# Places for the last z2 tiles, the rounding of the next tile's rows ahead of the norm, and the totals behind the third product, in one stage of an adaLN, S4 and gMLP kernel

## The chip, the cores and the metric

The kernel runs on one core of a Trainium2 chip. The time is the device time of one execution, in microseconds (us). Three runs of the kernel before took 1779.18, 1784.16 and 1779.81 us; their median is 1779.81 us. Smaller is better.

## The reference, cut to what matters

```python
h = _layernorm(x) * (1 + ca) + sa
x = x + ga * _A_ref(h, ...)              # S4: a long convolution along the 2048 rows
h = _layernorm(x) * (1 + cb) + sb
z = _gelu(einsum("bsd,df->bsf", h, w_in))        # 2048 x 576 by 576 x 4608
z1 = z[..., :Fh];  z2 = _layernorm(z[..., Fh:])  # Fh = 2304
g = einsum("ts,bsf->btf", w_sp, z2) + b_sp       # 2048 x 2048 by 2048 x 2304
x = x + gb * einsum("bsf,fd->bsd", z1 * g, w_out)
```

All arrays are float32. The kernel makes the large products of pairs of f16 numbers: a value is rounded to f16 ("hi"), and what is left over is rounded to f16 again ("lo"). The product by w_sp is made with fewer multiplications out of sums and differences of blocks, which is why half of z2's even tiles hold differences.

## The kernel before, in words

The program has three stages in a row: `ssm` (the S4 convolution and the first residual, about the first 440 us), `phase_a` (z2, up to about 683 us) and `phase_b` (z1, the product by w_sp, the product by w_out and the residual).

Phase A goes over the 2048 rows in 16 tiles b of 128 rows. The steps of one tile are small methods, and each puts its work on one engine:

- `turn(b)`: TensorE transposes the normalised rows n of tile b by five products into the PSUM tile `pt`, of which there is one.
- `turn_hi(b)`: ScalarE rounds `pt` to f16, into half of the tile `nt` (two instructions). `turn_lo(b)`: VectorE writes what is left over into the other half (two instructions), and GpSimd sends `nt` to DRAM for phase B (the transfer n_d). Three buffers `nt` take turns.
- `z2_mm(b, h)`, h = 0 to 4: the product of `nt` by 512 columns of w_in (256 for h = 4), 14 matmuls into a PSUM tile `pz`, of which there are six.
- `z2_gelu(b, h)`: ScalarE takes the gelu of `pz` into columns of the z2 tile, 128 x 2304 in float32. The z2 tile is taken from its pool at h = 0; before, three buffers take turns under the one name z2.
- `z2_stats(b, c)`: VectorE's statistics of 384 columns. `roots(b, x)`: VectorE's aggregation and a chain of 15 or so small instructions for the reciprocal root, for z2's tile b and for the rows of tile x. It ends with r and nm, the factor and the shift of the norm.
- `z2_diff(b)`, even tiles: VectorE subtracts one half of z2 from the other. `z2_norm(b)`: ScalarE applies the norm, in two instructions of 1152 columns on even tiles and one of 2304 on odd ones. `z2_store(b)`: two transfers from GpSimd's queue, z_d, send the tile to DRAM; when they have landed the place of the tile is free.
- `ln2_rows(b)`, `ln2_stats(b)`: VectorE's norm of the rows that a later tile will transpose.

Beside these the loop carries lists of side work for other weights, called by `do(b, k)`: loads, ScalarE's roundings, VectorE's sums and left-overs. The list PE holds products for totals, two matmuls of one column each into a `pz` tile, from which VectorE works out a scale (`sc`): `win_scale` at b = 1, 3, 5, 7, 9, `scales_sp` at 7 and `scales_out` at 14. Side loads `xz` bring blocks of w_sp, whose differences VectorE makes in place.

Each engine runs its instructions of phase A in the order in which the code issues them: `self.tied` wraps the engines so, and therefore all of them carry line 132, that of the wrapper. So an instruction that waits holds up all that stands behind it on its engine. For b above 2, the order in loop b before is, shortly: z2_mm(b, 0); gelu(b, 0); statistics of tile b-1's last columns; roots(b-1); diff; norm(b-1); ln2_rows(b+2); totals; z2_mm(b, 1); turn(b+1); gelu(b, 1); store(b-1); statistics; turn_hi(b+1); turn_lo(b+1); z2_mm(b, 2) and so on. For b = 3 this means that the first tile whose rounding stands behind a norm is tile 4; tiles 2 and 3 have it ahead.

After the loop come the statistics, roots, norm and store of tile 15, and phase A's buffers are handed back. Phase B begins with six units of z1 (`z1_unit`, matmuls L1415, gelu L1420). Then comes the first group of g_products (L1450 to L1452), whose operands `zset` are built from z2 as it lies in DRAM: loads `raw`, sums on VectorE (L1081 to L1083), hi on ScalarE (L1129), lo on VectorE (L1130). `g_unit` (L1465) adds its products up on VectorE, `out_products` (L1502 to L1505) is the product by w_out. Phase B's tiles lie where phase A's lay, and each waits for the last reader of what was there. In the built program the three z2 places lie at bytes 132544, 141760 and 150976 of a partition; The second and third tile z1 that phase B takes begin at bytes 134176 and 130080, 4096 bytes each, and so lie over the first place; its tiles gt and z1b begin at 138272 and 142368 and lie over the end of the first place and over the second. The first tile z1 lies elsewhere. Nothing of phase B lies at 150976. Before, tiles 12 and 15 are at the first place, 11 and 14 at the second, 13 at the third.

Of the kernel before, what the change touches and what calls it, by code (L numbers as in the profile page):

```python
# [9 lines left out]
F32 = mybir.dt.float32  # L10
# [12 lines left out]
FH = 2304  # L23
# [775 lines left out]
class Mlp:  # L799
# [419 lines left out]
    def z2_gelu(self, b, h):  # L1219
        n = min(512, FH - 512 * h)  # L1220
        if h == 0:
            self.zs[b] = self.zp.tile([128, FH], F32, name="z2")
            self.bz[b] = self.ap.tile([128, 6, 6], F32, name="bsz")
        self.nc.scalar.activation(self.zs[b][:, 512 * h:512 * h + n], self.pzs.pop((b, h))[:, :n], AF.Gelu_apprx_tanh,
                                  scale=self.wcol(5 + h, INV_IN))
# [24 lines left out]
    def phase_a(self):  # L1250
        self.prods, self.z1s, self.n2, self.bsp, self.gbs, self.wfs = {}, {}, {}, {}, {}, {}
        ap = self.ap = self.pool(self.c2, "ap", 2)
        cpa = ExitStack()
        self.pa = self.pool(cpa, "pa", 6, space=PSUM)
        self.ps1 = lambda: self.pa.tile([128, 512], F32, name="pz")
        self.zp = self.pool(self.c2, "zp", 3)
        self.wp = self.pool(self.ctx, "wp", 7, side="right")

        self.fp = self.pool(self.ctx, "fp", 1, side="right")
        self.wso = ap.tile([128, 4, 10, 128], F16, name="wso", bufs=1)  # L1260
        self.nc, plain = self.tied, self.nc
        self.nc.vector.memset(self.wso[64:, :, 9], 0.0)

        LD, PE, A0, A1, V0, V1 = range(6)
        sides = [[[] for _ in range(6)] for _ in range(17)]

        def side(b, k, fn, *a):
            sides[b][k].append((fn, a))

        def do(b, k):  # L1270
            for fn, a in sides[b][k]:
                fn(*a)

        for q in range(5):
            side(2 * q, LD, self.side_load, q)
            side(2 * q + 1, A0, self.side_sum, q)
            side(2 * q + 1, PE, self.win_scale, q)
            side(2 * q + 1, A1, self.side_hi, q)
            side(2 * q + 1, V1, self.side_last, q)
            side(2 * q + 1, V1, self.side_lo, q, 0)  # L1280
            side(2 * q + 2, V0, self.side_lo, q, 1)
        for h in range(2):
            side(1, LD, self.bsp_load, ap, h)
            side(2, A0, self.norm_bsp, h)
        for i in range(8):
            side(2 + i // 2, A1, self.wsp_load, 0, i, ap)
            side(3 + i // 2, A0, self.norm_sp, 0, i)
        for i in range(12):
            side(6 + i // 2, A1, self.out_load, ap, i)
            side(7 + i // 2, A0, self.norm_out, i)  # L1290
        for i in range(6):
            side(12 + i // 2, A1, self.wsp_load, 1, i, ap)
            side(13 + i // 2, A0, self.norm_sp, 1, i)
        side(13, V1, self.sums_out)
        side(14, PE, self.scales_out)
        side(6, V1, self.sums_sp, 0)
        side(7, PE, self.scales_sp, 0)
        side(11, PE, self.scales_gate, 0)
        for i in range(7):
            side(9 + i, V0, self.wsp_sums, i)  # L1300
            side(9 + i, A1, self.wsp_hi, 0, i)
            side(9 + i, V1, self.wsp_lo, 0, i)
            side(8 + i, V1, self.block_load, 0, i)
        side(10, LD, self.z1_rows, 0)
        side(11, LD, self.bias_load, 0)
        for f in (0, 9, 1):
            side(12, LD, self.z1_load, 0, f)

        self.turn(0)
        self.turn_hi(0)  # L1310
        self.x1_load(4)
        self.turn_lo(0)
        self.start_lo(3)
        do(0, LD)
        self.z2_mm(0, 0)
        self.start_sum(4)
        self.z2_gelu(0, 0)
        self.z2_mm(0, 1)
        self.win_scale(9)
        self.start_hi(4)  # L1320
        self.z2_gelu(0, 1)
        self.ln2_rows(1)
        self.z2_mm(0, 2)
        self.start_lo(4)
        self.z2_gelu(0, 2)
        self.z2_mm(0, 3)
        self.turn(1)
        self.turn_hi(1)
        self.z2_gelu(0, 3)
        self.turn_lo(1)  # L1330
        self.z2_mm(0, 4)
        self.ln2_stats(2)
        self.roots(x=2)
        self.ln2_rows(2)
        self.z2_stats(0, 0, 1, 2, 3)
        self.z2_gelu(0, 4)
        self.ln2_stats(3)
        self.z2_stats(0, 4)
        for b in range(1, 16):
            do(b, LD)  # L1340
            self.z2_mm(b, 0)
            do(b, A0)
            self.z2_gelu(b, 0)
            self.z2_stats(b - 1, 5)
            if b in (1, 2):
                do(b, PE)
                self.z2_mm(b, 1)
                self.turn(b + 1)
                self.z2_gelu(b, 1)
                self.turn_hi(b + 1)  # L1350
                self.turn_lo(b + 1)
            self.roots(b - 1, b + 2 if b + 2 < 16 else None)
            if b % 2:
                self.z2_diff(b - 1)
            self.z2_norm(b - 1)
            if b + 2 < 16:
                self.ln2_rows(b + 2)
            if b + 4 < 16:
                self.x1_load(b + 4)
            if b > 2:  # L1360
                if b > 3:
                    do(b, PE)
                self.z2_mm(b, 1)
                if b + 1 < 16:
                    self.turn(b + 1)
                self.z2_gelu(b, 1)
            self.z2_store(b - 1)
            do(b, V0)
            self.z2_stats(b, 0, 1)
            if 3 < b + 1 < 16:  # L1370
                self.turn_hi(b + 1)
                self.turn_lo(b + 1)
            self.z2_mm(b, 2)
            if b == 3:
                do(b, PE)
            self.z2_gelu(b, 2)
            do(b, A1)
            self.z2_mm(b, 3)
            self.z2_stats(b, 2, 3)
            self.z2_gelu(b, 3)  # L1380
            if b + 3 < 16:
                self.ln2_stats(b + 3)
            do(b, V1)
            self.z2_stats(b, 4)
            self.z2_mm(b, 4)
            self.z2_gelu(b, 4)
        cpa.close()
        self.z2_stats(15, 5)
        self.roots(15)
        self.z2_norm(15)  # L1390
        self.z2_store(15)
        self.nc = plain
        self.c2.close()
# [334 lines left out]
```

## Time and profile before

| | us |
|---|---|
| three runs | 1779.18, 1784.16, 1779.81 |
| profiled execution, its own time | 1783.02 |
| its span | 1781.2 |
| TensorE busy (matmuls) | 1693.0 |
| VectorE busy | 1119.1 |
| ScalarE busy | 785.2 |
| GpSimd busy | 223.9 |

The profile shows one execution. Its own time is 1.8 us over the span, for what lies before the first and behind the last instruction, and 3.2 us over the median of the runs. PE is TensorE, PEld its weight loads, DVE is VectorE, ACT ScalarE, POOL GpSimd and SP SyncE. PEclk is the share of its full clock that TensorE was granted. A timeline row gives start and length in us, engine, line, operation and tiles, and in brackets for how long the engine had stood idle and what ended that; a row of waits gives the sum in us, the number and the longest.

### The profile page before, as it was taken

The numbers are of one execution on the slowest core, as the hardware profiler recorded it, in microseconds if no ns is written. First come the engines' busy times: TensorE is split into PE (matmuls) and PEld (weight loads), VectorE is DVE, ScalarE is ACT, GpSimd is POOL, SyncE is SP. The second block draws the span as 40 slices with busy tenths as digits, with TensorE's granted clock in tenths as the row PEclk, the third lists the DMA queues.
The fourth block names the chain that finished last, engine by engine and source line by source line (L and its number), as shares of the span: only waits on it lengthen the run. The fifth ranks groups of instructions, "written<-read, shape, count | busy, mean of one in ns | idle before, by whom it ended". The sixth has DMA issues, their size and how long they took to land.

```text
span 1781.2 us, 33976 instructions
## 1 busy us (share of the span) xinstructions
PE 1693.0 (95%) x14202; PEld 1195.6 (67%) x14202; DVE 1119.1 (63%) x2182; ACT 785.2 (44%) x1023; POOL 223.9 (13%) x350
## 2 busy tenths in 40 slices
PE   5688999997999999999999999999999999999999
PEld 1344555565545555877787777887778787787787
DVE  7988999858899996988783544483222274222322
ACT  5669999854576665555351322241211132011110
POOL 1321222342122110000000000000000000000000
PEclk8788999998999999999999999999999999999999
DMA  8457545799598887876654666562655572555520
GB/s 277 140 206 236 144 129 162 188 250 303 165 289 285 268 237 227 288 277 241 222 204 154 246 238 222 204 254 101 217 203 188 176 271 70 182 173 175 201 84 28
DMA packets 145866, 361.57 MB, mean 203 GB/s; under 512 B 23296, under 2 KB 59008, under 8 KB 143792
## 3 DMA queue, kind: packets, MB, share of 16 engines
q1 hardware_dynamic: 103104, 167.30, 29.7%
q0 software_dynamic: 33120, 153.95, 25.8%
q10 hardware_dynamic: 9488, 38.16, 5.3%
q8 instruction: 111, 1.82, 0.4%
q14 instruction: 43, 0.35, 0.1%
HBM read 256.86 MB, written 93.05 MB: 196 GB/s over the span
## 4 chain that ended last, share of the span: by engine, by line
PE 59%; DVE 10%; issue 6%; DMA 4%; ACT 3%; SPq 0%; POOL 0%; ACTq 0%; DVEq 0%; POOLq 0%
PE ps L1452 10%; PE ps L1450 10%; PE ps L1451 10%; PE ps L1415 9%; PE pz L132 5%; PE ps L1505 3%; PE ps L1502 3%; PE ps L1504 3%; PE pk L132 2%; DVE zset L1130 2%; ACT z L132 1%; DVE gt L1465 1%; DMA gbs<-in_w_out 1%; DVE bsz L132 1%; DMA zset<-set_d 1%
## 5 line engine op out<-in xcount | busy, mean ns | idle before, releaser
L1450 PE MATMUL ps<-wsp,zset 128*128 128x256 f16 x2016 | 549.5, 273 | 6.3 <-DVE gt L1465 3.7
L1452 PE MATMUL ps<-wsp,zset 128*128 128x256 f16 x2016 | 549.5, 273 | 3.5 <-DVE zset L1130 3.4
L1451 PE MATMUL ps<-wsp,zset 128*128 128x256 f16 x2016 | 549.5, 273 | 0.0
L132 PE MATMUL pz<-wz,nt 128*128 128x512 f16 (+1 forms) x1120 | 224.7, 361 | 4.7 <-ACT nt L132 4.7
L1465 DVE SCALAR_TENSOR_TENSOR gt<-ps,sc,bsp 128x512 f32<-128x512 f32 x33 | 24.8, 750 | 316.4 <-PE ps L1452 316.4
L1415 PE MATMUL ps<-n2q,wf 128*128 128x512 f16 x1008 | 223.1, 379 | 0.0
L1450 PEld LDWEIGHTS <-zset 128*128 128x128 f16 x2016 | 197.5, 98 | 33.3 <-DVE gt L1465 4.3
L1452 PEld LDWEIGHTS <-zset 128*128 128x128 f16 x2016 | 197.3, 98 | 27.8 <-DVE zset L1130 4.9
L1451 PEld LDWEIGHTS <-zset 128*128 128x128 f16 x2016 | 197.3, 98 | 25.9
L132 PEld LDWEIGHTS <-nt 128*128 128x128 f16 x1120 | 110.1, 99 | 110.9 <-ACT nt L132 5.5
L1415 PEld LDWEIGHTS <-wf 128*128 128x128 f16 x1008 | 98.6, 98 | 111.7
L1427 POOL DMA_DIRECT2D zset<-set_d x96 | 50.8, 529 | 973.8 <-PE ps L1452 960.9
L1420 ACT ACTIVATE z<-ps,sc 128x512 f32<-128x512 f32 x56 | 37.9, 681 | 284.6 <-PE ps L1415 274.9
L1504 PE MATMUL ps<-wout,z 128*128 128x288 f16 x448 | 127.6, 286 | 0.0
L1505 PE MATMUL ps<-wout,z 128*128 128x288 f16 x448 | 127.6, 286 | 0.0
L1502 PE MATMUL ps<-wout,z 128*128 128x288 f16 x448 | 126.0, 286 | 0.9 <-ACT ot L1512 0.9
L1465 DVE SCALAR_TENSOR_TENSOR gt<-ps,sc,gt 128x512 f32<-128x512 f32 (+1 forms) x165 | 112.1, 696 | 5.4
L1130 DVE TENSOR_TENSOR zset<-raw,zset 128x1024 f16<-128x1024 f32 x48 | 58.7, 1224 | 84.3 <-ACT zset L1129 84.3
L1129 ACT ACTIVATE zset<-raw 128x1024 f16<-128x1024 f32 x48 | 50.3, 1050 | 95.8 <-PE ps L1452 55.5
L1520 DVE TENSOR_TENSOR ot<-ot,ps 128x288 f32<-128x288 f32 x31 | 14.0, 453 | 78.3 <-ACT ot L1512 78.3
L369 PE MATMUL ps<-ln_x,r1t 128*128 128x288 f32 x128 | 42.6, 491 | 19.2 <-ACT kab L437 8.0
L1512 ACT ACTIVATE ot<-ps 128x288 f32<-128x288 f32 x32 | 12.8, 408 | 106.2 <-PE ps L1502 88.1
(356 smaller groups left out, 2864.0 us busy)
## 6 DMA issues: line engine op xcount, KB each, us to landing
zset<-set_d POOLq DMA_DIRECT2D x96, 896.0 KB, 4.9
set_d<-zset ACTq DMA_DIRECT2D x36, 896.0 KB, 5.9
raw<-z_d SPq DMA_DIRECT2D x48, 512.0 KB, 4.7
wf<-win_d SPq DMA_DIRECT2D x72, 320.0 KB, 3.5
raw<-in_w_spT SPq DMA_DIRECT2D x43, 512.0 KB, 6.1
z_d<-z POOLq DMA_DIRECT2D x32, 576.0 KB, 7.9
u_d<-st1o POOLq DMA_DIRECT2D x16, 576.0 KB, 4.4
u<-u_d SPq DMA_DIRECT2D x36, 256.0 KB, 4.6
```

Source lines behind the costliest of these rows:

```text
L132: return self.tc.keep_in_program_order(f(*a, **k))
L1129: nc.scalar.activation(o[:, k, 0], t, AF.Copy)
L1130: nc.vector.tensor_tensor(o[:, k, 1], t, o[:, k, 0], op=ALU.subtract)
L1415: nc.tensor.matmul(pm.rearrange("p (t c) -> p t c", t=4), w[:, kw], self.n2[q][:, :, kn], start=i == 0, stop=i == len(Z1) - 1)
L1427: self.nc.gpsimd.dma_start(o, self.set_d[n // 4, n % 4])
L1450: T.matmul(pm, z[:, a, 0, c], w[:, b, 0], start=i + half == 0, stop=False, skip_group_check=True)
L1451: T.matmul(pm, z[:, a, 0, c], w[:, b, 1], start=False, stop=False, skip_group_check=True)
L1452: T.matmul(pm, z[:, a, 1, c], w[:, b, 0], start=False, stop=i == 7, skip_group_check=True)
L1465: V.scalar_tensor_tensor(dst, pm, inv, to, op0=ALU.mult, op1=ALU.add)
L1502: T.matmul(pl, p[:, 1, ts], w[:, 0, hs], start=st, stop=sp)
L1504: T.matmul(pa, p[:, 0, ts], w[:, 0, hs], start=st, stop=False)
L1505: T.matmul(pa, p[:, 0, ts], w[:, 1, hs], start=False, stop=sp)
```

## The change

The change does three things in phase A, and adds or drops no instruction.

First, the z2 tiles get names of their own, z20, z21 and z22, each with one buffer, and so a set place: tile b takes place b mod 3 up to tile 13, tile 14 takes place 0 and tile 15 place 2. In the built program the three places are the same three stretches of memory. After the change tiles 12 and 14 are at 132544, 13 at 141760, 11 and 15 at 150976. So tile 14 now follows tile 12 at its place (before: tile 11), and tile 15 follows tile 11 (before: tile 12).

Second, in the loop, the second product, the transposes of the next tile, the second gelu and `turn_hi(b+1)` stand ahead of the roots and the norm in all tiles (before: for b = 1 and 2 alone). `turn_lo(b+1)` stands behind roots and diff and ahead of norm and ln2_rows for b above 1 (before, for b above 2: behind two statistics of tile b).

Third, the totals of the PE list stand behind the third product for all b above 1 (before: ahead of the second product for b above 3).

```diff
@@ z2_gelu
-            self.zs[b] = self.zp.tile([128, FH], F32, name="z2")
+            self.zs[b] = self.zp.tile([128, FH], F32, name="z2%d" % (b % 3 if b < 14 else 2 * b - 28))
@@ phase_a
-        self.zp = self.pool(self.c2, "zp", 3)
+        self.zp = self.pool(self.c2, "zp", 1)
@@ phase_a, the loop over b
             self.z2_gelu(b, 0)
             self.z2_stats(b - 1, 5)
-            if b in (1, 2):
+            if b == 1:
                 do(b, PE)
-                self.z2_mm(b, 1)
+            self.z2_mm(b, 1)
+            if b + 1 < 16:
                 self.turn(b + 1)
-                self.z2_gelu(b, 1)
+            self.z2_gelu(b, 1)
+            if b + 1 < 16:
                 self.turn_hi(b + 1)
+            if b == 1:
                 self.turn_lo(b + 1)
             self.roots(b - 1, b + 2 if b + 2 < 16 else None)
             if b % 2:
                 self.z2_diff(b - 1)
+            if 2 < b + 1 < 16:
+                self.turn_lo(b + 1)
             self.z2_norm(b - 1)
             if b + 2 < 16:
                 self.ln2_rows(b + 2)
             if b + 4 < 16:
                 self.x1_load(b + 4)
-            if b > 2:
-                if b > 3:
-                    do(b, PE)
-                self.z2_mm(b, 1)
-                if b + 1 < 16:
-                    self.turn(b + 1)
-                self.z2_gelu(b, 1)
             self.z2_store(b - 1)
             do(b, V0)
             self.z2_stats(b, 0, 1)
-            if 3 < b + 1 < 16:
-                self.turn_hi(b + 1)
-                self.turn_lo(b + 1)
             self.z2_mm(b, 2)
-            if b == 3:
+            if b > 1:
                 do(b, PE)
             self.z2_gelu(b, 2)
```

The difference of the two programs on ScalarE, in loop b = 3 (z_5052 is the z2 of tile 2, z_5199 that of tile 3, and nt<-pt is the rounding of tile 4's rows; nm and r belong to tile 2's norm):

```order
-L132 ACTIVATE z_5199<-pz,sc 128x512
-L132 ACTIVATE z_5052<-z_5052,nm_5221,r_5220 128x1152
-L132 ACTIVATE z_5052<-z_5052,r_5220 128x1152
-L132 ACTIVATE z_5199<-pz,sc 128x512
-L132 ACTIVATE nt<-pt 128x512
-L132 ACTIVATE nt<-pt 128x128
+L132 ACTIVATE z_5199<-pz,sc 128x512 x2
+L132 ACTIVATE nt<-pt 128x512
+L132 ACTIVATE nt<-pt 128x128
+L132 ACTIVATE z_5052<-z_5052,nm_5246,r_5245 128x1152
+L132 ACTIVATE z_5052<-z_5052,r_5245 128x1152
 L132 ACTIVATE z_5199<-pz,sc 128x512
```

The second gelu of tile 3 and the rounding of tile 4 have moved from behind the two instructions of tile 2's norm to ahead of them; every later tile shows the same move.

VectorE before, in loop b = 14, from the end of tile 13's roots on (nm belongs to tile 13, z_6949 is the z2 of tile 14, nt<-pt is turn_lo of tile 15, sc<-pz begins what is worked out from the total of `scales_out`, and xz is a block of w_sp):

```order
L132 SCALAR_TENSOR_TENSOR nm_6972<-mvx,r_6971 128x1
L132 COPY sc<-pz 128x1
L132 TENSOR_SCALAR p2e<-sc 128x1
L132 TENSOR_SCALAR p2e<-p2e 128x1
L132 TENSOR_SCALAR sc<-p2e 128x1
L132 TENSOR_SCALAR sc<-sc 128x1
L132 TENSOR_TENSOR xz<-xz 128x256 x3
L1024 TENSOR_TENSOR sc<-sc 128x1
L132 TENSOR_TENSOR xz<-xz 128x256
L132 BN_STATS bsz<-z_6949 128x6 x2
L132 TENSOR_TENSOR nt<-pt,nt 128x512
L132 TENSOR_TENSOR nt<-pt,nt 64x128
```

and VectorE after, at the same place in the program (nm_6997 is tile 13's):

```order
L132 SCALAR_TENSOR_TENSOR nm_6997<-mvx,r_6996 128x1
L132 TENSOR_TENSOR nt<-pt,nt 128x512
L132 TENSOR_TENSOR nt<-pt,nt 64x128
L132 TENSOR_TENSOR xz<-xz 128x256 x4
L132 BN_STATS bsz<-z_6949 128x6 x2
L132 COPY sc<-pz 128x1
L132 TENSOR_SCALAR p2e<-sc 128x1
L132 TENSOR_SCALAR p2e<-p2e 128x1
L132 TENSOR_SCALAR sc<-p2e 128x1
L132 TENSOR_SCALAR sc<-sc 128x1
```

turn_lo of tile 15 has moved up to right behind the roots, past the block's differences and the two statistics, and the scale from the totals has moved down behind them.

On TensorE only the totals move, by two products, in the loops b = 5, 7, 9 and 14. On GpSimd's queue the transfer n_d of each tile from 4 on now stands ahead of the two z_d of the tile two before it. SyncE's order and the whole of phase B are as they were.

## The prediction

> **What bounds the kernel now.** I read the page first: how much of the span each engine works.
>
> ```profile
> span 1781.2 us, 33976 instructions
> PE 1693.0 (95%) x14202; PEld 1195.6 (67%) x14202; DVE 1119.1 (63%) x2182; ACT 785.2 (44%) x1023; POOL 223.9 (13%) x350
> ```
>
> TensorE (PE) works 95% of the span, so a reordering can win only what TensorE loses by waiting or by a low clock. The change touches phase A alone, from about 440 to 683 us, and through its end the start of phase B. So next the windows of TensorE, cut where it stood idle.
>
> ```profile
> core 0: us, PE busy (x), PEclk, DMA share, GB/s
> 440.00:497.40 57.40, 57.33 (x306) 1.00 0.59 191
> 497.40:501.10 3.70, 0.04 (x2) 0.87 0.71 201
> 501.10:510.10 9.00, 9.00 (x29) 0.67 0.96 316
> 693.20:696.80 3.60, 0.39 (x2) 1.00 0.00 0
> 696.80:800.00 103.20, 99.34 (x848) 1.00 0.79 280
> ```
>
> There is a hole in phase A, at 497.4, with a low granted clock in the 9 us behind it, and one at 693.2, where phase B's first set product waits. The timeline of TensorE names what ended the waits.
>
> ```profile
> 446.26 6.20 PE L132 MATMUL pz<-wz,nt 128*128 128x512 f16 x28
> 501.08 9.11 PE L132 MATMUL pz<-wz,nt 128*128 128x512 f16 x28 [3.66 <-ACT nt L132]
> 646.96 3.19 PE L132 MATMUL pz<-wz,nt 128*128 128x512 f16 x14 [0.32 <-ACT nt L132]
> 674.88 18.29 PE L1415 MATMUL ps<-n2q,wf 128*128 128x512 f16 x84
> 695.40 0.28 PE L1450 MATMUL ps<-wsp,zset 128*128 128x256 f16 x1 [2.23 <-ACT zset L1129]
> 696.80 0.28 PE L1452 MATMUL ps<-wsp,zset 128*128 128x256 f16 x1 [1.00 <-DVE zset L1130]
> ```
>
> The two phase A waits are for ScalarE's rounding of the next tile's rows (tiles 4 and 14); those in phase B are for the hi and then the lo half of the first set. ScalarE's timeline says why these came late.
>
> ```profile
> 497.48 1.35 ACT L132 ACTIVATE z<-z,nm,r 128x1152 f32<-128x1152 f32 x1 [2.47 <-DVE z L132]
> 500.45 0.75 ACT L132 ACTIVATE nt<-pt 128x512 f16<-128x512 f32 x2
> 682.26 2.31 ACT L132 ACTIVATE z<-z,nm,r 128x2304 f32<-128x2304 f32 x1 [5.44 <-DVE nm L132]
> 684.48 1.25 ACT L1420 ACTIVATE z<-ps,sc 128x512 f32<-128x512 f32 x2
> 692.99 0.69 ACT L1420 ACTIVATE z<-ps,sc 128x512 f32<-128x512 f32 x1 [7.26 <-DMA z_d<-z]
> 693.57 1.05 ACT L1129 ACTIVATE zset<-raw 128x1024 f16<-128x1024 f32 x1
> ```
>
> At 497.5 ScalarE stood idle for VectorE, did tile 2's norm, a gelu, and only then tile 4's rounding at 500.45. At the end it waits for VectorE's roots of tile 15, norms (682.26), does two gelus of z1, and waits 7.26 us for the store of tile 15, because the third gelu writes where tile 15 lies; the first set's rounding is queued behind it. So two engines set the seam: TensorE, which is done with z1 at 674.88 + 18.29 = 693.17, and the chain VectorE, norm(15), store, gelu, rounding, first lo at 696.7.
>
> VectorE itself is nearly never idle in phase A; this window has all engines, and the waits are all that VectorE has there.
>
> ```profile
> 466.00:682.00 216.00, 212.03 (x1111) 110.25 (x1110) 194.53 (x583) 144.07 (x211) 48.21 (x62) 0.98 0.81 255
> DVE bsz L132 <- ACT z L132: 4.0, 5, 1.3
> DVE xz L132 <- DMA xz<-in_w_spT: 1.8, 1, 1.8
> DVE nt L132 <- ACT nt L132: 1.4, 1, 1.4
> DVE wsp L132 <- ACT wsp L132: 0.7, 1, 0.7
> ```
>
> 194.53 us busy (third pair of numbers) and 4.0 + 1.8 + 1.4 + 0.7 = 7.9 us of named waits; the other 13.6 us go in steps between 583 instructions, which no reordering of these removes. So norm(15) can come earlier by a part of 7.9 us and no more.
>
> **The change part by part.** No instruction is added or removed, so every term is a wait.
>
> ```profile
> 481.26 1.02 DVE L132 TENSOR_TENSOR nt<-pt,nt 128x512 f16<-128x512 f32 x2 [1.40 <-ACT nt L132]
> 500.57 0.56 DVE L132 BATCH_NORM_STATS2 bsz<-z 128x6 f32<-128x384 f32 x1 [0.92 <-ACT z L132]
> 552.68 1.35 ACT L132 ACTIVATE z<-z,nm,r 128x1152 f32<-128x1152 f32 x1 [0.58 <-DVE z L132]
> ACT wso L132 <- DVE sc L132: 1.3, 1, 1.3
> ```
>
> *Rounding ahead of the norm, tile 4.* The second gelu and the rounding go into ScalarE's idle 2.47 us before 497.48: 0.69 for a gelu and 0.75 for the rounding are 1.44 us and fit there, so tile 4's hi is ready before TensorE wants it at 501.08 - 3.66 = 497.42. This removes 3.66 us idle and, as the hole goes, the slow stretch: 28 matmuls took 9.11 us there and 6.20 us at 446.26, so 2.91 us. By the Trainium skill, "TensorE: Matmul & The Clock Gate", section "What's actually happening", the array falls to half clock after about one idle window of some 3.4 us and is back after as much busy time; the trace agrees, with 3.66 us idle bringing 0.67 over the next 9 us and 2.23 us none of it. The lo half now stands behind roots and diff: VectorE's diff ended just before 497.48, and 1.0 us of lo follows; TensorE could wait for it between 0 and 1 us. I take 0, since hi products come first. With the 0.32 us at tile 14 TensorE's z1 units end 3.66 + 2.91 + 0.32 = 6.89 us earlier, at 686.28.
>
> *The same on VectorE.* turn_lo no longer comes behind statistics that wait for the late gelu. The first two rows above are the waits of that kind around tiles 3 and 4, and I let their 1.40 + 0.92 = 2.32 us go. ScalarE's spare time at a norm is under 1.44 us at one tile only, b = 7 (third row, 0.58 us), where VectorE may wait up to 0.86 us. At tile 15's rounding VectorE has the wait of 1.8 us for a block: turn_lo(15) waits in its place for about as long, and meanwhile the block comes. The bounds are 0 and all 7.9 us; I take 2.3, the two waits that the moved steps caused: norm(15) begins at 682.26 - 2.3 = 679.96.
>
> *The totals.* They go behind two more products on TensorE. A product takes 3.19 us, so the scale comes about 6.4 us later, and ScalarE's side rounding waits for it. Its users stand behind two gelus more, and VectorE's tiny chain behind statistics; I cost it at nothing; if that cover is gone, at the one wait of ScalarE for a scale that the trace shows in this stretch (fourth row), 1.3 us, in each of three loops (5, 7, 9).
>
> *GpSimd.* The transfer n_d now stands ahead of the two z_d. It waits for turn_lo, which is ahead of the norm, so nothing queues behind it that was ready; what it takes is hidden in the queue's long waits for the norm (the first three rows below).
>
> ```profile
> 646.32 2.01 POOL L132 DMA_DIRECT2D z_d<-z  x2 [11.51 <-ACT z L132]
> 673.52 2.00 POOL L132 DMA_DIRECT2D z_d<-z  x2 [10.51 <-ACT z L132]
> 685.02 2.02 POOL L132 DMA_DIRECT2D z_d<-z  x2 [9.49 <-ACT z L132]
> 686.04 6.84 DMA z_d<-z
> DMA to landing us min/median/max: 5.3/7.7/13.9
> ```
>
> *Set places.* The rows are the stores of tiles 12, 14 and 15, the second transfer of tile 15 from issue to landing, and the landings of all z_d from 472 to 690 us. z1's second tile now lies over tile 14's place. Its second transfer, issued a microsecond after the first, lands near 674.5 + 7.7 = 682.2, less the 2.3 us that VectorE gained: before the third gelu of z1, and that wait of 7.26 us goes. Then norm(15) at 679.96, the two gelus at 682.2, the third at 683.4, the rounding at 683.9 in place of 693.57: 9.7 us earlier. The first lo follows at the same distance, 3.23 us, at 687.1 in place of 696.80.
>
> *Sum.* TensorE is done with z1 at 686.28 and needs the first lo at 686.3 or so; it gets it at 687.1. TensorE gains 6.89 and its wait of 2.23 + 1.00 shrinks to about 0.8: in all 696.80 - 687.1 = 9.7 us. Behind that the order is the same, and the waits for lo halves from 700 to 900 us stay:
>
> ```profile
> PE ps L1452 <- DVE zset L1130: 2.4, 3, 1.3
> ```
>
> The profiled execution, 1783.02 us, becomes 1773.3; the median of the runs is 3.21 below the profiled one, so 1779.81 - 9.7 = **1770.1 us**. Bounds of this case: if VectorE gains nothing, 2.3 less (7.4 us, 1772.4); if it gains 3 or more, TensorE's 686.3 caps the start at 0.8 us more, and these 2.4 us might go too: 9.7 + 0.8 + 2.4 = 12.9 us, 1766.9.
>
> **The rivals.**
>
> *The place of tile 12 is not free in time.* gelu(14,0) writes over tile 12, whose second transfer, issued at about 647.3, landed 8.6 us later, the longest of these two:
>
> ```profile
> DMA to landing us min/median/max: 5.4/7.0/8.6
> 652.21 0.71 ACT L132 ACTIVATE z<-pz,sc 128x512 f32<-128x512 f32 x1
> ```
>
> The first row is of tile 12's transfers alone. gelu(14,0) ran at 652.21; it would now wait until 655.9. VectorE's wait for turn_lo(15) takes the place of the wait for the block, so my sum holds that much. With the longest landing of the stage, 13.9 us, it is 5.3 us more, VectorE and norm(15) come as much later, the rounding at 689.2, and the gain is 4.4 us: 1775.4. The Trainium skill, "Perfetto Trace Analysis", section "Identifying Performance Opportunities", says that gaps that repeat on the engine that should be full can mean too few buffers for the next tile; here that would be one gap, at tile 14, and no row of the kernel before shows ScalarE waiting for a z2 place. Chance 0.10.
>
> *The gain is given back or half made.* The first quarter of phase B is short of VectorE and of sets; set 3 needs tile 15's store, which moves by 2.3 us only, while TensorE wants it 9.7 us earlier. The read of z2 for a set takes 4.7 us:
>
> ```profile
> raw<-z_d SPq DMA_DIRECT2D x48, 512.0 KB, 4.7
> ```
>
> By my count the store lands at 685.02 - 2.3 + 1.0 + 6.84 = 690.6, set 3 is read by 695.3, its hi and first lo take the 3.23 us of set 0, 698.5, and the rest of it another microsecond. TensorE has three sets of 42 matmuls ahead of it, at 103.20 / 848 = 0.12 us each 15 us, so it wants set 3 at 702. If that fails, or if TensorE's hole at tile 4 stays, half is lost: 9.7 / 2 gives 1775.0; with the seam alone, 3.23 us, 1776.6. That is also the case in which the change doesn't do what it says. Chance 0.09.
>
> *Slower: VectorE waits for the rounding in every tile.* turn_lo now stands right behind roots (and diff), ahead of work that VectorE could do; if gelu and rounding come late there, because TensorE's second product or transposes or ScalarE's side work are late, VectorE loses up to 1.44 us a tile.
>
> ```profile
> ACT z L132 <- DVE nm L132: 31.7, 8, 5.4
> ACT z L132 <- DVE z L132: 29.7, 8, 8.7
> ```
>
> Against it: ScalarE waits 61.4 us in 16 norms, a mean of 3.8 us, so the room is there. With 12 tiles (b = 3 to 14) of 1.44 us and three loops of 1.3 us for the later totals it would cost 21.2 us of a VectorE that has no slack; less 2.3, norm(15) begins at 701.2, the rounding 3.94 us behind it as in my sum, at 705.1, 11.5 us later than before: 1791.3. It decides where the spare time at the norm is under 1.44 us in most tiles. Chance 0.07.
>
> **How the numbers follow.** My forecast has 0.74, the rivals 0.10, 0.09 and 0.07. The likeliest case's own range is 1766.9 to 1772.4; up to 1776.6 takes in the first two rivals and leaves out the slow one and what scatter there is. A measurement tells 0.3% from no change, 5.3 us here: faster means under 1774.5. So the two mild rivals are "same": 0.74 faster, 0.19 same, 0.07 slower.
>
> **What would show it.** Right: no wait of TensorE at tile 4 and clock 1.00 from 497 to 510; VectorE's waits in phase A near 5 us; the third z1 gelu with no wait for z_d; the first set product near 687 and the rest of phase B shifted whole. Wrong: a wait of ScalarE for z_d at tile 14 of more than 4 us, waits of VectorE for nt in many tiles, or new waits of TensorE for sets between 690 and 800 us.

## The result and the profile after

The changed kernel is slower, by about half a per cent: nine runs from 1784.16 to 1797.78 us with a median of 1791.86, against 1782.19 us for the kernel before in nine runs beside them; the ratio is 1.0051, 95% interval 1.0028 to 1.0074. The forecast was 1770.1 us and faster. Executions of one kernel scatter by 5 us and more to either side; and behind the S4 stage, which no edit touches, phase A began between 435.4 and 442.7 us in the twelve profiled executions. So below a stage is compared by distances inside an execution: from the transposes of tile 0 (line pt, the start of phase A on TensorE) to norm(15) on ScalarE, and to the first set product by a lo half on TensorE (the third set product, L1452 before and L1447 after).

The page of the changed kernel's profile, and behind it its windows of TensorE in phase A:

```profile
span 1787.0 us, 33982 instructions
PE 1696.9 (95%) x14202; PEld 1195.5 (67%) x14202; DVE 1117.7 (63%) x2182; ACT 785.2 (44%) x1023; POOL 223.8 (13%) x350
```

The windows, each with its length, TensorE's busy time and instructions, the granted clock, the share of the DMA engines and GB/s:

```profile
440.00:684.80 244.80, 232.39 (x1215) 0.99 0.80 235
504.90:516.70 11.80, 7.68 (x43) 1.00 0.91 300
516.70:524.60 7.90, 7.89 (x30) 0.78 0.61 164
```

Every engine works nearly as long as before; TensorE 3.9 us longer. From 440 us to z1's first matmul it takes 244.8 us in place of 234.9. The timeline of TensorE after shows the holes:

```profile
439.61 0.76 PE L132 MATMUL pt<-ident,n 128*128 128x128 f32 x5
493.71 10.75 PE L132 MATMUL pz<-wz,nt 128*128 128x512 f16 x56
516.71 7.89 PE L132 MATMUL pz<-wz,nt 128*128 128x512 f16 x28 [4.13 <-ACT nt L132]
563.85 9.41 PE L132 MATMUL pz<-wz,nt 128*128 128x256 f16 x42 [3.04 <-ACT z L132]
612.88 4.49 PE L132 MATMUL pz<-wz,nt 128*128 128x512 f16 x20 [1.32 <-DVE nt L132]
626.80 6.22 PE L132 MATMUL pz<-wz,nt 128*128 128x512 f16 x28 [1.32 <-ACT nt L132]
704.21 0.27 PE L1447 MATMUL ps<-wsp,zset 128*128 128x256 f16 x1
```

The hole at tile 4 is gone: TensorE runs on from 493.71. But there is one at tile 5, of 4.13 us and with a low clock behind it (0.78), and others follow. TensorE's step from one tile's transposes to the next is about 14.2 us for most tiles, but 20.1 and 20.2 us where the holes of 4.13 and 3.04 us lie, and 15.7 us twice later. The waits of VectorE and ScalarE over phase A and the seam tell why:

```profile
DVE nt L132 <- ACT nt L132: 18.6, 5, 8.0
ACT z L132 <- DVE nm L132: 18.0, 6, 5.4
ACT z L132 <- DVE z L132: 15.9, 3, 8.7
ACT wsst L132 <- DMA wsst<-in_w_spT: 15.2, 8, 4.7
ACT wsst L132 <- DMA wsst<-in_w_out: 15.1, 8, 3.8
ACT wso L132 <- DVE sc L132: 8.5, 4, 3.3
ACT wso L132 <- DMA wst<-in_w_in: 6.4, 1, 6.4
```

VectorE, which had no time to lose, now waits 18.6 us for ScalarE's roundings (1.4 before). ScalarE waits about half as long at its norms, and in place of that 30.3 us for the loads wsst, the blocks of weights whose squares it sums at the top of each loop (1.4 before), and 6.4 us for one more side load, wst (none before). One lap of what follows from that, as ScalarE's, SyncE's, VectorE's and again SyncE's timelines have it between tiles 4 and 5 (wsst is loaded from w_sp, x1t is the row buffer that ln2_rows frees, n<-x1t is ln2_rows):

```profile
498.78 0.34 SPq L132 DMA_DIRECT2D x1t<-x_d  x1
499.21 3.62 SPq L132 DMA_DIRECT2D wsst<-in_w_spT  x2
508.05 1.06 ACT L132 ACTIVATE wsst<-wsst 128x1024 f32<-128x1024 f32 x1 [2.96 <-DMA wsst<-in_w_spT]
513.87 1.06 ACT L132 ACTIVATE wsst<-wsst 128x1024 f32<-128x1024 f32 x1 [4.66 <-DMA wsst<-in_w_spT]
514.92 1.25 ACT L132 ACTIVATE z<-pz,sc 128x512 f32<-128x512 f32 x2
516.06 0.76 ACT L132 ACTIVATE nt<-pt 128x512 f16<-128x512 f32 x2
516.85 1.02 DVE L132 TENSOR_TENSOR nt<-pt,nt 128x512 f16<-128x512 f32 x2 [5.85 <-ACT nt L132]
517.90 0.82 DVE L132 SCALAR_TENSOR_TENSOR n<-x1t,mvx,mrow 128x576 f32<-128x576 f32 x1
518.75 0.34 SPq L132 DMA_DIRECT2D x1t<-x_d  x1
519.19 0.94 SPq L132 DMA_DIRECT2D wsst<-in_w_spT  x2
```

It is a ring. On SyncE the row load of tile b+4 stands ahead of the side loads, and it waits until ln2_rows(b+2) has read the buffer, so the side loads leave only then. Behind their squares on ScalarE stand both gelus and the rounding; turn_lo on VectorE waits for that; and behind turn_lo, since the change, stands the next ln2_rows, which frees the next row load. This lap took 518.75 - 498.78 = 20.0 us. The two laps behind it took 13.4 and 14.0 us (the next row loads leave at 532.17 and 546.20), the third 20.8 (566.95). TensorE's own step is 14.2 us, so even a quick lap leaves little room to make up for a slow one.

The ring does not say why this lap was slow. The loads did not leave late: before, the same pair left at 498.57, which is 60.0 us behind the first transposes, and after it left at 499.21, 59.6 us behind them. They landed late. The first row is SyncE's before; the two others are the landings of wsst that left between 496 and 515 us, four transfers before and two after:

```profile
498.57 0.90 SPq L132 DMA_DIRECT2D wsst<-in_w_spT  x2
DMA to landing us min/median/max: 5.1/5.7/6.8
DMA to landing us min/median/max: 8.8/10.4/12.0
```

The other slow lap began in the same way: its pair left at 546.65 and took 13.7 and 15.0 us to land (the pair of that loop before, 6.4 and 8.6), while the pairs in between took 5.6 to 7.5. So each of the two losses of some 6 us began with loads that landed slowly, and the new order of VectorE let them hold up the engine that has no time to lose. Why they landed slowly is not shown.

The seam went as forecast. ScalarE's timeline:

```profile
669.44 1.26 ACT L132 ACTIVATE z<-pz,sc 128x512 f32<-128x512 f32 x2 [3.33 <-DMA z_d<-z]
695.56 2.31 ACT L132 ACTIVATE z<-z,nm,r 128x2304 f32<-128x2304 f32 x1 [5.44 <-DVE nm L132]
697.77 1.82 ACT L1415 ACTIVATE z<-ps,sc 128x512 f32<-128x512 f32 x3
```

The third gelu of z1 follows the first two with no wait for a store, and TensorE runs into the first set product without one. But norm(15) stands 695.56 - 439.61 = 255.95 us behind the first transposes, before 682.26 - 438.61 = 243.65: 12.3 us later. The first lo product is 704.21 - 439.61 = 264.6 us behind them, before 696.80 - 438.61 = 258.2: the 12.3 us, less the 5.9 that the seam saved, are 6.4.

### The profile page after: what moved, and what is told of

Read it like the earlier page. It is cut to its first block, busy times and chain, and to the rows that moved or that the text cites. A ratio compares the mean times of both kernels' runs of the same rounds, so it can differ in the third digit from the quotient of the medians.

```text
span 1787.0 us, 33982 instructions
## 1 busy us (share of the span) xinstructions
PE 1696.9 (95%) x14202; PEld 1195.5 (67%) x14202; DVE 1117.7 (63%) x2182; ACT 785.2 (44%) x1023; POOL 223.8 (13%) x350
## 4 chain that ended last, share of the span: by engine, by line
PE 48%; DVE 5%; issue 5%; DMA 4%; ACT 1%; SPq 0%; ACTq 0%; DVEq 0%; POOLq 0%
PE ps L1445 9%; PE ps L1446 9%; PE ps L1410 9%; PE ps L1447 9%; PE ps L1500 3%; PE ps L1497 3%; PE ps L1499 3%; DVE zset L1130 2%; DVE gt L1460 1%; DMA zset<-set_d 1%; PE pz L132 1%; DMA raw<-z_d 1%; DMA gbs<-in_w_out 1%; ACT zset L1129 1%; DMA raw<-in_w_out 1%
## 5 line engine op out<-in xcount | busy, mean ns | idle before, releaser
L1447 PE MATMUL ps<-wsp,zset 128*128 128x256 f16 x2016 | 549.5, 273 | 3.0 <-DVE zset L1130 3.0
L132 PE MATMUL pz<-wz,nt 128*128 128x512 f16 (+1 forms) x1120 | 225.9, 361 | 11.9 <-ACT nt L132 7.0
L1447 PEld LDWEIGHTS <-zset 128*128 128x128 f16 x2016 | 197.2, 98 | 26.9 <-DVE zset L1130 4.1
L369 PE MATMUL ps<-ln_x,r1t 128*128 128x288 f32 x128 | 41.5, 480 | 20.1 <-issue 12.8
## 6 DMA issues: line engine op xcount, KB each, us to landing
u<-u_d SPq DMA_DIRECT2D x36, 256.0 KB, 4.6
```

The source lines that it names most:

```text
L132: return self.tc.keep_in_program_order(f(*a, **k))
L1447: T.matmul(pm, z[:, a, 1, c], w[:, b, 0], start=False, stop=i == 7, skip_group_check=True)
```

## The experiments

Theory RING is that turn_lo ahead of ln2_rows closes the ring above. Its rivals were that the later totals hold ScalarE up (TOTALS) and that n_d and z_d side by side crowd the DMA engines, so that loads land slowly (QUEUE). Each run was timed in five rounds against the kernel before.

| run | ratio to before, 95% interval | norm(15), us behind first transposes | first lo product, us behind them | VectorE waits for nt | ScalarE waits for wsst |
|---|---|---|---|---|---|
| before | | 243.7 | 258.2 | 1.4 | 1.4 |
| changed | 1.0051 (1.0028 to 1.0074) | 256.0 | 264.6 | 18.6 | 30.3 |
| 1 turn_lo put back | 0.9960 (0.9946 to 0.9974) | 245.1 | 256.1 | 0 | 11.9 |
| 2 totals put back | 1.0045 (1.0025 to 1.0066) | 258.6 | 271.2 | 8.6 | 31.4 |
| 3 side work behind rounding | 0.9973 (0.9959 to 0.9988) | 245.9 | 253.2 | 1.9 | 6.7 |
| 4 before, tile 4 and places | 0.9990 (0.9975 to 1.0005) | 246.6 | 257.3 | 1.4 | 10.7 |
| 5 changed, side loads first | 0.9936 (0.9918 to 0.9954) | 239.0 | 248.2 | 1.9 | 1.2 |
| 6 rotation put back | 1.0066 (1.0044 to 1.0089) | 259.4 | 273.8 | 20.9 | 34.6 |
| 7 before, shifted places | 0.9963 (0.9949 to 0.9977) | 245.8 | 256.7 | 1.4 | 5.2 |
| 8 run 1, loads first, shifted places | 0.9938 (0.9921 to 0.9954) | 240.3 | 250.9 | 0 | 0 |
| 9 before, side loads first | 0.9993 (0.9976 to 1.0010) | 242.7 | 257.3 | 1.4 | 0 |
| 10 run 5, shifted places | 0.9953 (0.9935 to 0.9971) | 240.7 | 249.3 | 2.6 | 0 |

The ratio stands on 6 to 12 executions of each version, the other columns on one profiled execution each (waits from 466 us to the end of phase A; the 21.8 us that the expectations give for nt in the changed kernel are those of the whole of phase A).

**1. turn_lo put back behind ln2_rows.**

```diff
-            if 2 < b + 1 < 16:
+            if b == 2:
                 self.turn_lo(b + 1)
...
             self.z2_stats(b, 0, 1)
+            if 3 < b + 1 < 16:
+                self.turn_lo(b + 1)
             self.z2_mm(b, 2)
```

> The changed kernel with turn_lo (and its transfer n_d) of tiles 4 to 15 put back behind ln2_rows, the stores and the two statistics; rounding on ScalarE, set places and totals stay as changed. Theory RING: VectorE's turn_lo ahead of ln2_rows closes a ring: ln2_rows frees the row buffer, only then SyncE issues the row load and behind it the side loads, these land 6 to 14 us later, ScalarE's side work at the top of the next loop waits for them, behind it stand the gelus and the rounding, and turn_lo waits for that. With turn_lo behind ln2_rows the ring is open: VectorE's waits for nt fall from 21.8 us to under 5, TensorE has no hole of over 1.5 us in phase A, norm(15) starts near 681 to 683 in place of 695.6, and the time is 6 to 11 us under the kernel before (ratio about 0.995). Rival TOTALS: the later totals hold up ScalarE's side rounding (8.5 us of waits for the scale), and the rounding of rows stands behind it: this run stays within 3 us of the changed kernel, 5 to 10 us over the one before.

The time is 7 us under the kernel before, in the range that RING gave, and VectorE's waits for nt went to nothing. Two points of the expectation failed: norm(15) was not earlier than before, and TensorE kept a wait of 2.4 us, for a rounding behind side loads that were late still: n_d stands behind z_d again here, as before, and still side loads took up to 15.3 us to land. So the order of n_d and z_d is not needed for a slow landing, which speaks against QUEUE; and with turn_lo behind ln2_rows VectorE no longer waits for the rounding behind it; its longest wait in phase A is 4.3 us for a gelu. VectorE's waits in this run, up to the first set:

```profile
DVE bsz L132 <- ACT z L132: 5.6, 3, 4.3
DVE zset L1130 <- ACT zset L1129: 3.9, 1, 3.9
DVE xz L132 <- DMA xz<-in_w_spT: 3.6, 2, 2.9
DVE wsp L132 <- ACT wsp L132: 0.7, 1, 0.7
```

**2. The totals put back.**

```diff
-            if b == 1:
+            if b == 1 or b > 3:
                 do(b, PE)
             self.z2_mm(b, 1)
...
-            if b > 1:
+            if b == 3:
                 do(b, PE)
```

> The changed kernel with the totals ahead of the second product again for b above 3, as before. Theory TOTALS: the four waits of ScalarE for the scale (1.6 to 3.3 us) go, VectorE's waits for nt fall with them to under 8 us, and the time is no higher than that of the kernel before (ratio 1.000 or less). Theory RING: the waits of ScalarE for the side loads (30 us) and of VectorE for nt (about 20 us) stay, and the time stays 5 to 10 us over the kernel before (ratio about 1.004).

TOTALS falls: the run is as slow as the changed kernel. ScalarE's waits for the scale did go from 8.5 to 1.6 us, and VectorE's for nt fell to 8.6, where RING had them stay at about 20, a miss; but TensorE took the wait over, as its totals now stood ahead of a product and waited for sums that ScalarE makes of the late loads. TensorE's and ScalarE's waits:

```profile
PE pz L132 <- ACT wso L132: 11.2, 2, 6.0
ACT wsst L132 <- DMA wsst<-in_w_spT: 18.3, 9, 5.5
ACT wsst L132 <- DMA wsst<-in_w_out: 13.1, 8, 3.1
ACT wso L132 <- DVE sc L132: 1.6, 1, 1.6
```

**3. ScalarE's side work behind the rounding.**

```diff
-            do(b, A0)
+            if b == 1:
+                do(b, A0)
             self.z2_gelu(b, 0)
...
                 self.turn_hi(b + 1)
+            if b > 1:
+                do(b, A0)
```

> The changed kernel with ScalarE's side work at the top of the loop (squares and sums of side loads) moved behind the rounding of the next tile's rows, for b above 1; VectorE's order, n_d, totals and places stay as changed. Theory RING: gelu and rounding no longer stand behind the side loads, so the ring is open at another place: VectorE's waits for nt fall to under 6 us, norm(15) starts before 684, and the time is 5 to 11 us under the kernel before (ratio about 0.995). Rival QUEUE: the loads are slow because n_d and z_d now go out side by side and crowd the DMA engines; as the transfers stay as they are, TensorE's holes of 3 to 4 us stay, and the time stays 4 to 10 us over the kernel before.

The waits for nt and the holes of 3 us are gone: cut at ScalarE, the ring is open too. This does not decide between RING and QUEUE, as the expectation meant it to: with the squares behind the rounding, a slow load no longer holds up the rounding, whatever makes it slow, and side loads took up to 14.8 us to land here. The measured gain, 0.27% or some 4 to 5 us, is at or just under the low end of the 5 to 11 us expected, and norm(15) is 2.2 us later behind the first transposes than before.

**4. The two terms of the sum alone, on the kernel before.**

```diff
-            if b in (1, 2):
-                do(b, PE)
+            if b in (1, 2, 3):
+                if b < 3:
+                    do(b, PE)
                 self.z2_mm(b, 1)
                 self.turn(b + 1)
                 self.z2_gelu(b, 1)
                 self.turn_hi(b + 1)
+            if b in (1, 2):
                 self.turn_lo(b + 1)
...
+            if b == 3:
+                self.turn_lo(b + 1)
             self.z2_norm(b - 1)
```

(with the set places of the change)

> The kernel before with two parts of the change alone: the set places, and for b = 3 alone the second product, gelu and rounding ahead of the norm with turn_lo of tile 4 behind the diff. All tiles from 5 on as before, totals as before. My sum for the change rested on these two terms: TensorE's hole at tile 4 (6.6 us with its half clock) and the wait of z1's third gelu (7.3 us). If the terms were right and only the other tiles spoiled them, the hole at tile 4 is gone, z1's third gelu does not wait for a store, and the time is 7 to 10 us under the kernel before (ratio 0.994 to 0.996). If the ring bites at tile 4 alone, or tile 14 waits long for the place of tile 12, the gain is under 3 us.

The small gain cannot be told from none, which is the last case of the expectation. The hole at tile 4 moved to tile 5, as this row of TensorE's timeline has it, and tile 14's first gelu waited for the store of tile 12, as ScalarE's row below it shows:

```profile
516.91 4.88 PE L132 MATMUL pz<-wz,nt 128*128 128x512 f16 x14 [3.44 <-ACT nt L132]
661.13 0.69 ACT L132 ACTIVATE z<-pz,sc 128x512 f32<-128x512 f32 x1 [4.19 <-DMA z_d<-z]
```

So TensorE's hole at tile 4 was not a fault of that tile alone: what was taken out there came back one tile later. Ahead of tile 5's rounding ScalarE waited 3.53 us for a side load: its pair took 5.5 and 9.9 us to land, before 5.1 and 6.8.

**5. The row load behind the side loads.** One line of the changed kernel moves on SyncE's queue:

```diff
-            if b + 4 < 16:
-                self.x1_load(b + 4)
             self.z2_store(b - 1)
...
             do(b, A1)
+            if b + 4 < 16:
+                self.x1_load(b + 4)
             self.z2_mm(b, 3)
```

> The changed kernel with one line moved: the row load x1_load(b+4) stands on SyncE's queue behind the loop's side loads, no longer ahead of them. Everything on TensorE, VectorE, ScalarE and GpSimd stays as changed, turn_lo ahead of ln2_rows included. Theory RING: the side loads no longer wait for ln2_rows, so this too opens the ring: ScalarE's waits for side loads fall from 30 us to under 8, VectorE's waits for nt from 21.8 to under 6, and the time is 4 to 10 us under the kernel before (ratio about 0.996). Rival: VectorE waits for the rounding because gelu and rounding themselves are late (1.4 us a tile), or because the loads are slow in landing, not late in starting: then VectorE's waits for nt stay above 15 us and the time stays 4 to 10 us over the kernel before.

1772.03 us against 1784.27, the lowest ratio of all, and more than the 4 to 10 us expected. The order on TensorE, VectorE, ScalarE and GpSimd is that of the changed kernel; only the time at which the side loads start is another. What SyncE waits for shows it, in the changed kernel:

```profile
SPq L132 <- DVE n L132: 132.9, 10, 31.9
SPq L132 <- DVE wsp L132: 45.2, 6, 9.7
```

and with the line moved, where the loads wait for their own buffers, which ScalarE's squares free:

```profile
SPq L132 <- ACT wsst L132: 61.6, 14, 25.2
SPq L132 <- DVE n L132: 50.1, 10, 6.6
```

The loads of the lap above leave at 491.19 there in place of 499.21, ScalarE does both squares with no wait, and TensorE's timeline has no hole left up to z1 but the 0.7 us ahead of tile 0's first product, which every version has. The loads did not land faster here: wsst took 5.5 to 12.3 us, with a median of 8.2, against 4.3 to 15.0 and 7.1 in the changed kernel. So the run shows that late side loads are what the change pays for, and that an earlier start cures it; it does not show that a late start was the fault. These are the load, TensorE's start of phase A, norm(15) and the first lo product:

```profile
491.19 1.68 SPq L132 DMA_DIRECT2D wsst<-in_w_spT  x2
439.36 0.77 PE L132 MATMUL pt<-ident,n 128*128 128x128 f32 x5
678.40 2.31 ACT L132 ACTIVATE z<-z,nm,r 128x2304 f32<-128x2304 f32 x1 [5.44 <-DVE nm L132]
687.56 0.27 PE L1447 MATMUL ps<-wsp,zset 128*128 128x256 f16 x1
```

**6. The rotating buffers put back.**

```diff
-            self.zs[b] = self.zp.tile([128, FH], F32, name="z2%d" % (b % 3 if b < 14 else 2 * b - 28))
+            self.zs[b] = self.zp.tile([128, FH], F32, name="z2")
```

(and three buffers in the pool)

> The changed kernel with the three rotating z2 buffers of before; the order stays as changed. Tile 15 then lies under z1's second tile again. Theory PLACES WORK: the third z1 gelu waits again some 7 us for tile 15's store behind a norm(15) that is as late as in the changed kernel or 3 us earlier (no wait of 3.3 us for tile 12's place): the first set's lo comes about 13.5 us behind norm(15), TensorE waits 3 to 7 us at the seam, and the time is 2 to 6 us over the changed kernel (ratio to before 1.006 to 1.009). Rival PLACES HURT: the wait at tile 14 costs more than the seam gives: this run is 2 us or more under the changed kernel.

PLACES WORK holds in the profile: TensorE waits 2.43 us for the hi half and 1.00 for the lo, and the lo product comes 711.26 - 437.48 = 273.8 us behind the first transposes. In the times the difference to the changed kernel, 0.15%, is within the intervals.

```profile
709.87 0.28 PE L1445 MATMUL ps<-wsp,zset 128*128 128x256 f16 x1 [2.43 <-ACT zset L1129]
711.26 0.39 PE L1447 MATMUL ps<-wsp,zset 128*128 128x256 f16 x1 [1.00 <-DVE zset L1130]
```

**7. Set places alone, in another map.**

```diff
+            self.zs[b] = self.zp.tile([128, FH], F32, name="z2%d" % (b if b < 3 else (1, 0, 2)[b % 3]))
```

(in place of the name z2, with one buffer each, in the kernel before)

> The kernel before with set places alone, in another map: from tile 3 on, tiles 15, 12, 9, 6, 3 lie at the second place, 13, 10, 7, 4 at the first, 14, 11, 8, 5 at the third, so no late tile follows one that is only two tiles older; order as before. By my sum the seam alone is worth what TensorE waits there, 2.23 + 1.00 us, since z1's units end where they did: no wait of z1's third gelu, no wait of TensorE for the first set, 2 to 4 us under the kernel before (ratio about 0.998). If the earlier set lets later waits of the first quarter go as well, up to 6 us.

Faster, by 0.23 to 0.51%, which is 4 to 9 us, where 2 to 4 were expected and 6 at most. ScalarE takes three gelus of z1 in a row and TensorE has no wait at the seam; the hole at tile 4 is there, in this execution with 5.07 us:

```profile
506.58 8.40 PE L132 MATMUL pz<-wz,nt 128*128 128x512 f16 x28 [5.07 <-ACT nt L132]
690.73 1.82 ACT L1420 ACTIVATE z<-ps,sc 128x512 f32<-128x512 f32 x3
```

**8. Both cuts of the ring, and the other map.** The edits of runs 1, 5 and 7 on the changed kernel.

> A version from what was seen: the changed kernel with turn_lo behind ln2_rows and the statistics as in the first experiment, the row load behind the side loads, and the places of the map in which no late tile follows one two tiles older. If the ring was the cause and both cuts add, ScalarE's waits for side loads fall under 5 us, TensorE has no wait over 1 us in phase A, and the time is 8 to 13 us under the kernel before (ratio 0.993 to 0.9955), below the first experiment. If one cut is enough, it is equal to the first experiment within 2 us.

As expected, ScalarE's waits for wsst are gone, TensorE has no wait over 1 us in phase A, and the time is 10.8 us under the kernel before. The ratio, 0.9938, is under run 1's, with intervals that just overlap, and equal to that of run 5. Run 10 differs from this run in turn_lo alone, and has 0.9953. So with the side loads first, putting turn_lo back adds nothing that can be measured.

**9. The side loads first, in the kernel before.** The edit of run 5 on the order of before.

> The kernel before with one line moved: the row load x1_load(b+4) behind the side loads of the loop on SyncE's queue; order of all other engines, totals and z2 buffers as before. In the kernel before ScalarE waits only 1.4 us for side loads, so theory RING says that the loads were late only where turn_lo stood ahead of ln2_rows: TensorE's hole at tile 4 (rounding behind the norm) and the wait of z1's third gelu stay, and the time is within 3 us of the kernel before (ratio 0.998 to 1.001). Rival: the late side loads were a general brake that the change only made visible; then this run gains 5 us or more, and the move of one line, not the order of the change, made the gain of the fifth experiment.

No difference, as RING has it. The same line that is worth 1.1% between the changed kernel and run 5 is worth nothing here, where late loads cost nothing to begin with: ScalarE's waits for wsst were 1.4 us before and are none now, and the hole at tile 4 and the waits at the seam stay:

```profile
501.47 6.22 PE L132 MATMUL pz<-wz,nt 128*128 128x512 f16 x28 [3.65 <-ACT nt L132]
694.88 0.28 PE L1450 MATMUL ps<-wsp,zset 128*128 128x256 f16 x1 [2.52 <-ACT zset L1129]
```

**10. Run 5 with the other map.**

> The changed kernel with the row load behind the side loads (as in the fifth experiment) and the map of places in which no late tile follows one two tiles older. In the fifth experiment ScalarE still waited 3.2 us at tile 14 for tile 12's store; TensorE had no wait there. If that wait costs nothing, since VectorE has its own wait for the block of w_sp at that place, the time is equal to the fifth experiment's ratio of 0.9936 within 0.0015. If it costs, this is 2 to 3 us faster (ratio about 0.992).

0.9953 is 0.0017 over 0.9936, just outside the 0.0015 of the expectation and in the direction of slower, but the intervals overlap. The wait for tile 12's place at tile 14 cost nothing that can be seen, and its removal brought nothing.

## Why the prediction was wrong

**The step that failed is the one on VectorE.** The prediction took turn_lo's move ahead of ln2_rows as a gain of 2.3 us, with a cost only where ScalarE's spare time at a norm is under the 1.44 us of a gelu and a rounding. That spare time, 61.4 us in 16 norms, was read as room (and it was short at one tile more than the prediction said: at b = 5 ScalarE waited 1.36 us). But it lies behind ScalarE's side work in the loop, and the rounding now waits with that side work; room behind a wait does not help what stands ahead of it. What decides is when the side loads land: ScalarE waited 30.3 us for wsst and 6.4 for wst, VectorE 18.6 us for the rounding, and norm(15) came 12.3 us later, where the prediction had 2.3 us earlier. And the side loads leave behind a row load that waits for VectorE. The prediction's rows of the kernel before did not hold SyncE's waits; its trace has them, 121.2 us in ten waits for VectorE's ln2_rows:

```profile
SPq L132 <- DVE n L132: 121.2, 10, 33.3
```

SyncE's order was the same before and after, and so it was not costed. From the first slow lap on its times were not the same: the instruction that releases it had been put behind a new wait, and so one slow landing made all that followed later. Runs 1, 3 and 5 open the ring at three different places, VectorE, ScalarE and SyncE, and each is faster than the kernel before. Strictly, runs 1 and 3 stretch the ring: in their order, as in the kernel before, a late load holds up the ln2_rows of one tile later, so that a lap has the time of two tiles.

**The slow rival had the place but not the price.** It said that turn_lo would wait right behind the roots in every tile for 1.44 us, and gave 1791.3 us; measured were 1791.86. The agreement is chance: VectorE's waits from 466 us on were five, of up to 8.0 us, and came from loads. The row that was quoted against it, ScalarE's waits at the norms, was the wrong row to ask.

**The two terms of the sum.** TensorE's 6.9 us: the hole at tile 4 did go, but came back at tile 5 (4.13 us and 7.89 us for matmuls that take 6.20), and run 4 shows that curing tile 4 alone moves it too. The seam: right; the wait of z1's third gelu went, and runs 6 and 7 show it apart. With the ring open, in run 5, both terms come in: TensorE is done with z1 6.4 us earlier, where the sum had 6.9, the first lo product is 248.2 us behind the first transposes in place of 258.2, 10.0 us, where the sum had 9.7, and norm(15) is 4.6 us earlier, where it had 2.3.

**The other steps.** The totals at nothing: the waits for the scale did come, 8.5 us, so the cover was gone, but run 2 shows that their old place costs as much in this order. GpSimd's n_d at nothing: right as far as run 5 shows, which keeps it ahead of z_d. The rival on tile 12's place: ScalarE waited 3.33 us there, TensorE 0.89 behind it, and runs 5 and 10 show no difference with and without. Set 3 at the seam and the first quarter of phase B gave nothing back that shows: from the first lo product to the end the changed kernel's profiled execution is 1788.77 - 704.21 = 1084.6 us, before 1783.02 - 696.80 = 1086.2.

**What stays open.** Why side loads sometimes take 12 to 15 us to land in place of 5 to 8, and whether the change makes that more frequent: one profiled execution of each version cannot tell, and run 7, with the order of before, has landings of up to 13.1 us. Why run 3 gained less than runs 5 and 8, and why runs 1 and 7 gained more in time than the 2.1 and 1.5 us by which their first lo product is earlier, was not settled either; the scatter of executions is as large as these differences, and the profiled executions of runs 1 and 7 were the slowest of theirs.

## What to carry to other kernels

When an instruction is moved on an in-order engine, follow what stands behind it to the queue that it releases: a DMA queue whose order is unchanged still starts later if its head waits for what was moved. Spare time of an engine is room only for work that stands between that engine's last wait and it; ask of each wait on that engine whether the moved work now lies behind it. And before a step is moved ahead, look for a ring, from the step through buffer, load and side work back to the step, and put loads that need nothing ahead of loads that wait. A load's time to land is no fixed sum, 4.3 to 15.0 us for one kind of load in one stage here: an engine that has no time to lose should not stand behind it without a margin.

## What the runs showed of the hardware

A hole of nearly the same length on TensorE did not always bring a low clock: after 3.66 us idle in the kernel before 28 matmuls took 9.11 us, after 3.65 us idle in run 9 the same 28 took 6.22. After 4.13 us and 5.07 us (the changed kernel, run 7) they took 7.89 and 8.40. Shorter holes brought it too: after 2.44 us in run 1 the 28 took 7.90, with a granted clock of 0.56 over the first 3.1 us, and after 3.04 us in the changed kernel the clock was 0.59 over 4.15 us; after 2.23 us at the seam before it stayed at 1.00. So the 2.91 us that the prediction counted for the clock could not be counted on in a hole of that length. "TensorE: Matmul & The Clock Gate" of the Trainium skill, section "What's actually happening", has a window of some 3.4 us that runs freely, and the half clock after at least one idle window. The two outcomes behind holes of 3.65 and 3.66 us agree with a window that runs freely; the low clock behind holes of 2.44 and 3.04 us, shorter than that window, does not agree with the rule as the page states it.
